# Attention and feed-forward of one chip core: two phases in sequence, or interleaved by hand per batch

## The chip, the core and the metric

The kernel runs on one core of one Trainium2 chip. The core has a matrix engine (PE, with its weight loads shown apart as PEld), a vector engine (DVE), a scalar engine (ACT), a general engine (POOL) and a queue engine (SP) that starts the transfers (DMAs) between the chip's large memory and the core's on-chip memories. Each engine works through its own list of instructions in order and waits at semaphores for the others. The metric is the time of one execution on the device in microseconds (us); smaller is better.

## The reference

Two stages, 4 batches of 768 tokens each, 8 heads of 64 numbers.

```python
q_bits = einsum('bhsd,dk->bhsk', q, proj) > 0        # 6 hash bits per query, the same for keys
mask   = q_bucket[:, :, :, None] == k_bucket[:, :, None, :]
scores = where(mask, 0.125 * q @ k.T, -1e9)          # 768 x 768 per head
attn   = softmax(scores) @ v                         # 768 x 64 per head
x      = attn as (3072 tokens, 512)                  # heads side by side
ffn    = (gelu(x @ w_gate) * (x @ w_val)) @ w_out    # 512 -> 1536 -> 512
out    = x + sigmoid(x @ w_res) * ffn
```

So a query attends only to keys whose 6 bits all equal its own. The kernel (both versions) gets the mask without comparing: the bits are appended to q and k as extra rows of the contraction, scaled so that one bit that differs lowers the exponent far enough for exp to give nothing.

## The kernel before

Every name and line is one of the listing below. The attention comes first, for all four batches, then the feed-forward for all 3072 tokens; the output of the attention, `x_sb`, stays on the chip in between, with the 512 features on the partitions.

For each head, q and k are loaded as 6 tiles of 128 tokens, transposed on PE in fp32 (L104, 6 transposes per side into one PSUM tile `ap`), copied out by ACT (L106), multiplied by `proj` (L109: the 128 tokens are the stationary operand, only 6 columns stream), turned into signs by ACT (L112), transposed again (L116) and copied below the 64 features (L117). DVE makes the bf16 versions (L119, L121). All the PSUM tiles of this preparation have the tag `ap` in a pool with one buffer, so that each step waits until the one before has been copied out.

Then, for each of 6 key tiles `jt`: scores with the keys on the partitions (L134, 512 and 256 queries), exp on ACT in two pieces (L138), and the product with v (L141), v being stationary (65 columns: 64 features and a column of ones that gives the softmax's sum) and the exponentials streaming. The output `ot` has features on the partitions and 768 queries along the row; the sums lie in one row, whose reciprocal (L148) DVE takes on one partition. POOL copies it to 64 partitions (L149) and DVE multiplies (L153).

The feed-forward works on 512 tokens at a time: gate and value products per 128 of the 1536 inner features (L191, L197), GELU on ACT (L194), product on DVE (L199), the gate of the residual (L205, L207 sigmoid), the output product (L213) with features on the partitions, and at the end 16 transposes back (L222, copied by ACT at L223) before the rows are stored (L224). The weights are loaded and cast to bf16 on DVE (L168, L169) when the attention's buffers are given back.

The order of the instructions on each engine is set by a scheduler, from the order of the code and the buffers of the pools. All DMAs go through SP's queue.

## Time and profile before

| | us |
|---|---|
| median of 3 runs | 804.09 (801.24 to 804.7) |
| profiled execution, span from its first to its last instruction | 793.3 |
| its attention, to the last exp | 0 to 534 |
| weights arriving, feed-forward starting | 534 to 600 |
| feed-forward for the rest | 600 to 793 |

| engine | busy us (share of the span) | instructions |
|---|---|---|
| PE | 712.2 (90%) | 3360 |
| PEld | 412.1 (52%) | 3360 |
| DVE | 325.4 (41%) | 383 |
| ACT | 409.0 (52%) | 845 |
| POOL | 37.5 (5%) | 40 |

No time of the profiled execution other than its span is printed; the median of the runs is 10.8 us above that span. Busy time of PE is counted from the start of a matmul to its modelled end, and matmuls overlap: a PE that is busy all the time can still have idle columns. The clock that the throttle granted to PE ("PEclk", 1.00 is full) belongs beside every PE duration: the same matmul streams half as fast at 0.50. The mean over this execution is 0.754. A name such as `sp<-q_aug_bf,k_aug_bf` is output and inputs of an instruction, "PE L134" a line of the listing.

### The profile page before, as it was taken

The page shows a single profiled execution, that of the slowest core. Times are in us where ns is not written, and L with a number is a line of the kernel's source. Part 1 is how long each engine was busy: PE and PEld are TensorE (multiplying, and loading weights), DVE is VectorE, ACT ScalarE, POOL GpSimd, SP SyncE. Part 2 cuts the span into 40 slices and gives each one's busy share as a digit, 9 for nine tenths or more (in the row PEclk, how much of TensorE's full clock was granted, in tenths as well). Part 3 has the DMA queues.
Part 4 walks back from the last instruction along what each step waited for, and adds up shares of the span by engine and source line. Part 5 has one row for each costly group of instructions (what it writes and reads, how often), then busy time and mean ns, then how long its engine had stood idle before and what let it go on. Part 6 is the DMA issues. An engine that isn't in the chain of part 4 may idle for free.

```text
span 793.3 us, 8913 instructions
## 1 busy us (share of the span) xinstructions
PE 712.2 (90%) x3360; PEld 412.1 (52%) x3360; DVE 325.4 (41%) x383; ACT 409.0 (52%) x845; POOL 37.5 (5%) x40
## 2 busy tenths in 40 slices
...
PEclk9965557865567785557675655555899999999997
...
GB/s 141 58 40 41 40 41 30 41 41 40 40 40 39 32 51 40 40 41 30 40 31 31 0 1 1 0 0 283 154 85 61 1 54 0 54 12 43 32 22 54
DMA packets 82299, 36.24 MB, mean 46 GB/s; under 512 B 76112, under 2 KB 76112, under 8 KB 82256
## 3 DMA queue, kind: packets, MB, share of 16 engines
...
## 4 chain that ended last, share of the span: by engine, by line
PE 78%; ACT 10%; issue 6%; DMA 4%; DVE 2%; ACTq 0%; POOL 0%; DVEq 0%; POOLq 0%
PE bp L109 17%; PE ot L141 13%; PE ap L104 10%; PE sp L134 10%; PE fps L213 7%; PE gps L191 7%; PE vps L197 7%; ACT e L138 5%; PE sp_raw L116 5%; DMA tmp<-in_moe_w_out_dram 3%; PE rps L205 2%; ACT k_aug_bf L117 2%; DMA out_dram<-o_row 1%; PE tp L222 1%; ACT q_aug_bf L117 1%
## 5 line engine op out<-in xcount | busy, mean ns | idle before, releaser
L138 ACT ACTIVATE e<-sp,exp_bias_sb 128x512 bf16<-128x512 f32 (+1 forms) x384 | 206.8, 577 | 61.6 <-PE sp L134 57.3
L148 DVE RECIPROCAL recip<-ot 1x512 f32<-1x512 f32 x64 | 160.9, 2532 | 141.9 <-PE ot L141 141.9
L141 PE MATMUL ot<-e,v_aug 128*65 128x512 bf16 (+1 forms) x384 | 166.4, 458 | 26.8 <-ACT e L138 26.8
L134 PE MATMUL sp<-q_aug_bf,k_aug_bf 70*128 70x512 bf16 (+1 forms) x384 | 153.6, 454 | 0.0
L194 ACT ACTIVATE gtmp<-gps 128x512 bf16<-128x512 f32 x72 | 42.9, 597 | 109.8 <-PE gps L191 109.2
L191 PE MATMUL gps<-x_sb,t 128*128 128x512 bf16 x288 | 81.0, 392 | 11.4 <-DVE t L169 9.8
L134 PEld LDWEIGHTS <-k_aug_bf 70*128 70x128 bf16 x384 | 50.3, 131 | 71.8 <-issue 61.3
L197 PE MATMUL vps<-x_sb,t 128*128 128x512 bf16 x288 | 78.5, 389 | 5.8 <-DVE t L169 5.8
L109 PEld LDWEIGHTS bp<-proj_sb,q_aug 64*128 64x128 f32 x384 | 68.8, 271 | 17.5 <-ACT q_aug L106 17.1
L199 DVE TENSOR_TENSOR hh<-gtmp,vps 128x512 bf16<-128x512 bf16 x72 | 49.3, 687 | 69.1 <-PE vps L197 59.9
L141 PEld LDWEIGHTS <-v_aug 128*65 128x65 bf16 x384 | 56.4, 147 | 38.9 <-issue 23.5
L109 PE MATMUL bp<-proj_sb,q_aug 64*128 64x6 f32 x384 | 71.7, 316 | 1.5 <-ACT q_aug L106 1.5
L109 PEld LDWEIGHTS bp<-proj_sb,k_aug 64*128 64x128 f32 x384 | 61.1, 244 | 17.7 <-ACT k_aug L106 17.7
L213 PE MATMUL fps<-hh,t 128*128 128x512 bf16 x288 | 64.7, 382 | 4.3 <-DVE t L169 4.2
L109 PE MATMUL bp<-proj_sb,k_aug 64*128 64x6 f32 x384 | 64.0, 296 | 1.6 <-ACT k_aug L106 1.6
L112 ACT ACTIVATE sgn_t<-bp 128x36 bf16<-128x36 f32 x64 | 12.8, 200 | 94.6 <-PE bp L109 94.6
L149 POOL PARTITION_BROADCAST recip<-recip x32 | 36.4, 1137 | 495.6 <-DVE recip L148 495.6
L104 PE MATMUL ap<-ident,q_s 128*64 128x128 f32 x192 | 46.7, 403 | 14.5 <-POOL ident masks.py:199 9.0
L121 DVE CAST k_aug_bf<-k_aug 64x768 bf16<-64x768 f32 x32 | 18.0, 562 | 83.4 <-ACT k_aug L106 83.4
L191 PEld LDWEIGHTS <-t 128*128 128x128 bf16 x288 | 27.6, 100 | 43.0 <-issue 8.8
L104 PE MATMUL ap<-ident,k_s 128*64 128x128 f32 x192 | 46.7, 405 | 3.4 <-ACT q_aug_bf L117 3.4
L197 PEld LDWEIGHTS <-t 128*128 128x128 bf16 x288 | 27.9, 99 | 40.8 <-DVE t L169 10.1
(34 smaller groups left out, 473.0 us busy)
## 6 DMA issues: line engine op xcount, KB each, us to landing
q_s<-in_q_dram SPq DMA_DIRECT2D x32, 192.0 KB, 2.6
k_s<-in_k_dram SPq DMA_DIRECT2D x32, 192.0 KB, 2.6
v_tmp<-in_v_dram SPq DMA_DIRECT2D x32, 192.0 KB, 3.0
out_dram<-o_row SPq DMA_DIRECT2D x24, 256.0 KB, 2.0
tmp<-in_moe_w_gate_dram SPq DMA_DIRECT2D x4, 768.0 KB, 4.2
tmp<-in_moe_w_val_dram SPq DMA_DIRECT2D x4, 768.0 KB, 4.2
tmp<-in_moe_w_out_dram SPq DMA_DIRECT2D x12, 256.0 KB, 2.7
tmp<-in_moe_w_res_dram SPq DMA_DIRECT2D x4, 256.0 KB, 2.7
```

Source lines behind the costliest of these rows:

```text
L104: nc.tensor.transpose(ap[:D, bass.ts(t, 128)], ten_s[:, t, :], ident)
L109: nc.tensor.matmul(bp[:, t * NBITS:(t + 1) * NBITS], ten_aug[0:D, bass.ts(t, 128)], proj_sb, start=True, stop=True)
L116: nc.tensor.transpose(sp[:NBITS, bass.ts(t, 128)], sgn[:, t, :], ident_bf)
L134: nc.tensor.matmul(sp[:, :nsz], k_aug_bf[0:KAUG, bass.ts(jt, 128)], q_aug_bf[0:KAUG, n0:n0 + nsz], start=True, stop=True)
L138: nc.scalar.activation(e[:, n0:n0 + nsz], sp[:, :nsz], AF.Exp, scale=exp_scale, bias=exp_bias_sb)
L141: nc.tensor.matmul(ot[:, :nsz], v_aug[:, jt, :], e[:, n0:n0 + nsz], start=(jt == 0), stop=(jt == ST - 1))
L148: nc.vector.reciprocal(recip[0:1, n0:n0 + nsz], ot[D:D + 1, :nsz])
L191: nc.tensor.matmul(gps, wg[:, kk, bass.ts(m, P)], x_bf[:, kk, :], start=(kk == 0), stop=(kk == KM - 1))
L194: nc.scalar.activation(gtmp, gps, AF.Gelu)
L197: nc.tensor.matmul(vps, wv[:, kk, bass.ts(m, P)], x_bf[:, kk, :], start=(kk == 0), stop=(kk == KM - 1))
L199: nc.vector.tensor_mul(hh[:, m, :], gtmp, vps)
L213: nc.tensor.matmul(fps, wo[:, kk, bass.ts(m, P)], hh[:, kk, :], start=(kk == 0), stop=(kk == KF - 1))
```

## The change

The kernel is written anew around one loop, and its instructions now stand in the order of the code (`manual_schedule`), not in that of a scheduler.

- **Order.** For each batch b the loop makes 48 steps (8 heads x 6 key tiles). A step issues the scores and the exp of its key tile, then perhaps a piece of the preparation of a later pair of heads, then one or two pieces of the feed-forward of batch b-1 (7 pieces in 4 steps; a batch has 48), and last the product with v of the key tile two steps back. After the 48 steps come 24 transposes of x and the 24 gate products with GELU of batch b; the feed-forward of the last batch stands alone at the end.
- **Preparation** works on a pair of heads. Tokens are loaded 6 neighbours to a partition. Two tiles of 64 features are transposed at once (12 fp32 transposes of 128x128 per pair in place of 24 of 128x64). The hash is one product per head and side with `proj` stationary in 32 columns and 384 token columns streaming (fp32), each of the four on its own 32 columns of PE, that is, on its own 32 output partitions. DVE compares with zero, and 8 small DMAs carry the bit rows below the features (L170).
- **Product with v** (L196): the exponentials are stationary (six 128x128 loads per key tile) and 65 columns of v stream. Tokens are on the partitions, so that the sums are a column: DVE takes 6 reciprocals per partition (L205) and one multiplication (L206). The one-partition reciprocal and the POOL broadcast are gone. `av` has one PSUM buffer.
- **Exp** runs once per key tile over 768 columns without a bias operand (L186); scores have two buffers.
- **Feed-forward** in halves of 384 tokens. Residual gate and output product now give tokens on the partitions (L242, L249), so that the final transposes and their copies are gone; x itself is transposed instead (L215). Sigmoid is written as tanh.
- **Weights** are loaded during batch 0, one transfer every third step, and cast on POOL (L134).

On **SP** the queue at the program's start, before:

```order
L57 DMA proj_sb<-in_proj_dram 64x6
L86 DMA q_s<-in_q_dram 128x6x64
L87 DMA k_s<-in_k_dram 128x6x64
L88 DMA v_tmp<-in_v_dram 128x6x64
L86 DMA q_s<-in_q_dram 128x6x64
```

and now (`aug` is the tile of one head with q and k side by side, `bits` the hash bits of a pair of heads):

```order
L75 DMA proj_pair<-in_proj_dram 64x6
L76 DMA proj_pair<-in_proj_dram 64x6
L101 DMA qs<-in_q_dram 128x2x384
L101 DMA ks<-in_k_dram 128x2x384
L101 DMA vs<-in_v_dram 128x2x384
L170 DMA aug_107<-bits 6x384 x4
L170 DMA aug_110<-bits 6x384 x4
L101 DMA qs<-in_q_dram 128x2x384
```

The loads of one head after the other stood back to back; now the loads of the second pair stand behind the eight transfers that wait for the first pair's hash bits.

On **PE** one key tile in the middle of the attention, before (preparation of later heads between the scores and the product with v):

```order
L134 LDWEIGHTS k_aug_bf
L134 MATMUL sp<-q_aug_bf,k_aug_bf 128x512
L134 LDWEIGHTS k_aug_bf
L134 MATMUL sp<-q_aug_bf,k_aug_bf 128x256
L104 MATMUL ap<-ident,k_s 64x128 x6
L141 LDWEIGHTS v_aug
L141 MATMUL ot<-e,v_aug 65x512
```

and now, at the start of batch 1's steps, behind the last gate product of batch 0 (buffer numbers kept):

```order
L223 MATMUL gps_1287<-xT_1114,wg_147 128x384
L183 LDWEIGHTS aug8_131
L183 MATMUL sc_1293<-aug8_131 128x512
L184 LDWEIGHTS aug8_131
L184 MATMUL sc_1293<-aug8_131 128x256
L233 LDWEIGHTS wv_148
L233 MATMUL vps_1298<-xT_1114,wv_148 128x384
```

Value products of batch 0 now follow the scores of batch 1 on PE, ahead of that key tile's product with v; before, the first product of the feed-forward on PE (L191) stood behind the last one of the attention (L141).

On **ACT**, the same stretch, now (before, all exps of the program came first, then GELU and sigmoid in turns with a table load at each):

```order
L186 ACTIVATE e<-sc 128x768 x16
L225 ACT_TABLE_LOAD
L225 ACTIVATE gh<-gps 128x384 x24
L186 ACT_TABLE_LOAD
L186 ACTIVATE e<-sc 128x768 x6
L152 COPY trT<-tps 128x512
L186 ACTIVATE e<-sc 128x768 x2
L245 ACTIVATE th<-rps 128x512
L186 ACTIVATE e<-sc 128x768 x2
```

Exps, copies of the preparation and tanhs share one order on ACT, and the list holds 8 table loads, two per batch.

The core of the diff (setup, buffers and what is only removed are left out; the removed code is in the listing above):

```diff
+    ctx.enter_context(tc.manual_schedule())
...
+    e_pool = ctx.enter_context(tc.tile_pool(name="e", bufs=6))
+    sc_psum = ctx.enter_context(tc.tile_pool(name="sc_psum", bufs=2, space=PSUM))
+    av_psum = ctx.enter_context(tc.tile_pool(name="av_psum", bufs=1, space=PSUM))
+    mm_psum = ctx.enter_context(tc.tile_pool(name="mm_psum", bufs=3, space=PSUM))
...
+    NAUG = 12
+    augs = []
+    for i in range(NAUG):
+        a = const.tile([P, 2 * S], BF16, name=f"aug{i}")
+        nc.vector.memset(a[D:KAUG, 0:S], 1.0)
+        nc.vector.memset(a[D:KAUG, S:2 * S], -0.25 * NBITS)
+        augs.append(a)
...
+    def load_pair(b, j):
+        for nm, src in (("q", q), ("k", k), ("v", v)):
+            s = stage.tile([P, 2, T, D], FP32, tag=nm + "s", name=nm + "s")
+            nc.sync.dma_start(
+                s, src[b, 2 * j:2 * j + 2].rearrange("h (p t) d -> p h t d", t=T))
+            staged[(nm, b, j)] = s
...
+    def load_weight():
+        nxt = next(weight_gen, None)
+        if nxt is None:
+            return
+        dst, src, parts = nxt
+        tmp = wstage.tile([P, DFF], FP32, tag="wtmp", name="wtmp")
+        if parts is None:
+            view = tmp
+        else:
+            view = tmp[:, :parts * DMODEL].rearrange("p (c d) -> p c d", c=parts)
+        nc.sync.dma_start(view, src)
+        nc.gpsimd.tensor_copy(dst, view)
...
+    def prep_pair(b, j):
+        qs, ks, vs = (staged.pop((nm, b, j)) for nm in "qkv")
+        va = vaugs[b % NVA]
+        nc.gpsimd.tensor_copy(va[:, 2 * j:2 * j + 2, :, 0:D], vs)
+        trT = tr_pool.tile([P, 2 * S], FP32, tag="trT", name="trT")
+        tiles = [s[:, hh, 2 * t2:2 * t2 + 2, :].rearrange("p t d -> p (t d)")
+                 for hh in range(2) for s in (qs, ks) for t2 in range(T // 2)]
+        for g in range(3):
+            ps = mm_psum.tile([P, 512], FP32, tag="mm", name="tps")
+            for i in range(4):
+                nc.tensor.transpose(ps[:, i * P:(i + 1) * P], tiles[4 * g + i], ident)
+            if g == 1:
+                nc.vector.tensor_copy(trT[:, g * 512:(g + 1) * 512], ps)
+            else:
+                nc.scalar.copy(trT[:, g * 512:(g + 1) * 512], ps)
+            yield
+        hp = mm_psum.tile([P, 512], FP32, tag="mm", name="hps")
+        for i in range(4):
+            nc.tensor.matmul(hp[32 * i:32 * i + 32, 0:CH], proj_pair, trT[:, i * CH:(i + 1) * CH],
+                             start=True, stop=True)
+        bits = s_pool.tile([P, CH], BF16, tag="bits", name="bits")
+        nc.vector.tensor_scalar(bits, hp[:, 0:CH], 0.0, 0.5, op0=ALU.is_gt, op1=ALU.subtract)
+        for hh in range(2):
+            a = aug_of(b, 2 * j + hh)
+            for par in range(2):
+                nc.vector.tensor_scalar_mul(
+                    a[0:D, :].rearrange("d (s n) -> d s n", s=2)[:, :, par * CH:(par + 1) * CH],
+                    trT[par * D:(par + 1) * D, hh * S:(hh + 1) * S].rearrange("d (s n) -> d s n", s=2),
+                    QKS)
+            for side in range(2):
+                for par in range(2):
+                    row = 32 * (2 * hh + side) + NBITS * par
+                    nc.sync.dma_start(
+                        a[D:D + NBITS, side * S + par * CH:side * S + (par + 1) * CH],
+                        bits[row:row + NBITS, :])
+        yield
...
+    def scores(b, h, jt):
+        a = aug_of(b, h)
+        sp = sc_psum.tile([P, 1024], FP32, tag="sc", name="sc")
+        lhsT = a[0:KAUG, S + jt * P:S + (jt + 1) * P]
+        nc.tensor.matmul(sp[:, 0:512], lhsT, a[0:KAUG, 0:512], start=True, stop=True)
+        nc.tensor.matmul(sp[:, 512:S], lhsT, a[0:KAUG, 512:S], start=True, stop=True)
+        e = e_pool.tile([P, S], BF16, tag="e", name="e")
+        nc.scalar.activation(e, sp[:, 0:S], AF.Exp, scale=EXPS)
+        e_tiles[(b, h, jt)] = e
+    def attend(b, h, jt):
+        e = e_tiles.pop((b, h, jt))
+        if jt == 0:
+            av_tiles[(b, h)] = av_psum.tile([P, 512], FP32, tag="av", name="av")
+        av = av_tiles[(b, h)]
+        va = vaugs[b % NVA]
+        for t in range(T):
+            nc.tensor.matmul(av[:, t * DV:t * DV + D + 1], e[:, t * P:(t + 1) * P], va[:, h, TS[jt], :],
+                             start=(jt == 0 and t == 0), stop=(jt == T - 1),
+                             skip_group_check=True)
+        if jt == T - 1:
...
+            o = av[:, 0:T * DV].rearrange("p (t d) -> p t d", d=DV)
...
+            rec = s_pool.tile([P, T, 1], FP32, tag="rec", name="rec")
+            nc.vector.reciprocal(rec, o[:, :, D:D + 1])
+            nc.vector.tensor_mul(x_tok[b][:, :, h * D:(h + 1) * D], o[:, :, 0:D],
+                                 rec.to_broadcast([P, T, D]))
+    def transpose_x(b):
+        xT[b] = x_pool.tile([P, KM, S], BF16, tag="xT", name="xT", bufs=1)
+        for ko in range(KM):
+            ps = mm_psum.tile([P, 1024], BF16, tag="mm", name="xps")
+            for t in range(T):
+                nc.tensor.transpose(ps[:, t * P:(t + 1) * P], x_tok[b][:, t, ko * P:(ko + 1) * P], ident_bf)
+            nc.vector.tensor_copy(xT[b][:, ko, :], ps[:, 0:S])
+    def gate(b, m, c):
+        if m == 0:
+            gh[(b, c)] = h_pool.tile([P, KF, CH], BF16, tag="gh", name="gh", bufs=3)
+        ps = mm_psum.tile([P, 512], FP32, tag="mm", name="gps")
+        for kk in range(KM):
+            nc.tensor.matmul(ps[:, 0:CH], wg[:, kk, m * P:(m + 1) * P], xT[b][:, kk, c * CH:(c + 1) * CH],
+                             start=(kk == 0), stop=(kk == KM - 1))
+        nc.scalar.activation(gh[(b, c)][:, m, :], ps[:, 0:CH], AF.Gelu)
+    def feed_forward(b):
+        for c in range(2):
+            for m in range(KF):
+                ps = mm_psum.tile([P, 512], FP32, tag="mm", name="vps")
+                for kk in range(KM):
+                    nc.tensor.matmul(ps[:, 0:CH], wv[:, kk, m * P:(m + 1) * P],
+                                     xT[b][:, kk, c * CH:(c + 1) * CH],
+                                     start=(kk == 0), stop=(kk == KM - 1))
+                sl = gh[(b, c)][:, m, :]
+                nc.vector.tensor_mul(sl, ps[:, 0:CH], sl)
+                yield 4 * CH
+            for t in range(c * T // 2, (c + 1) * T // 2):
+                rps = mm_psum.tile([P, 512], FP32, tag="mm", name="rps")
+                for kk in range(KM):
+                    nc.tensor.matmul(rps, xT[b][:, kk, t * P:(t + 1) * P], wr[:, kk, :],
+                                     start=(kk == 0), stop=(kk == KM - 1))
+                th = o_pool.tile([P, DMODEL], BF16, tag="th", name="th")
+                nc.scalar.activation(th, rps, AF.Tanh, scale=0.5)
+                yield 4 * 512
+                ops = mm_psum.tile([P, 512], FP32, tag="mm", name="ops")
+                for kk in range(KF):
+                    nc.tensor.matmul(ops, gh[(b, c)][:, kk, (t - c * T // 2) * P:(t - c * T // 2 + 1) * P], wo[:, kk, :],
+                                     start=(kk == 0), stop=(kk == KF - 1))
+                    if kk % 4 == 3 and kk < KF - 1:
+                        yield 4 * 512
+                y = o_pool.tile([P, DMODEL], FP32, tag="y", name="y")
+                nc.vector.scalar_tensor_tensor(y, th, 1.0, ops, op0=ALU.add, op1=ALU.mult)
+                o = o_pool.tile([P, DMODEL], FP32, tag="o", name="o")
+                nc.vector.scalar_tensor_tensor(o, y, 0.5, x_tok[b][:, t, :], op0=ALU.mult, op1=ALU.add)
+                nc.sync.dma_start(
+                    out[b * S:(b + 1) * S, :].rearrange("(p t) d -> p t d", t=T)[:, TS[t], :], o)
+                yield 4 * 512
+    for j in range(NPAIR):
+        load_pair(0, j)
+        if j < 2:
+            for _ in prep_pair(0, j):
+                pass
...
+    for b in range(B):
+        todo = list(preps) if b == 0 else []
+        if b + 1 < B:
+            todo += [(b + 1, j) for j in range(NPAIR)]
+        loads = [x for x in todo if x[0] > 0]
...
+        for i in range(nsteps + LEAD):
+            if i < nsteps:
+                scores(b, *bsteps[i])
+            if i % 3 == 0:
+                load_weight()
+            if loads and i % 8 == 2:
+                load_pair(*loads.pop(0))
+            if prep_gen is None and todo and i >= 4 and todo[0] not in loads:
+                prep_gen = prep_pair(*todo.pop(0))
+            if prep_gen is not None and (b == 0 or i % 2 == 1):
+                if not run(prep_gen):
+                    prep_gen = None
+            if ff is not None:
+                run(ff)
+                if i % 4 != 0:
+                    run(ff)
+            if i >= LEAD:
+                attend(b, *bsteps[i - LEAD])
+        while prep_gen is not None or todo:
+            if prep_gen is None:
+                if todo[0] in loads:
+                    load_pair(*loads.pop(0))
+                prep_gen = prep_pair(*todo.pop(0))
+            if not run(prep_gen):
+                prep_gen = None
+        while ff is not None and run(ff):
+            pass
+        transpose_x(b)
+        for c in range(2):
+            for m in range(KF):
+                gate(b, m, c)
+        ff = feed_forward(b)
+    while run(ff):
+        pass
```

220 lines of the change are left out of this document (64 added, 156 removed).

## The prediction

> **What bounds the kernel now.** I read the page first: the slices, then the chain of waits.
>
> ```profile
> PEclk9965557865567785557675655555899999999997
> PE 78%; ACT 10%; issue 6%; DMA 4%; DVE 2%; ACTq 0%; POOL 0%; DVEq 0%; POOLq 0%
> PE bp L109 17%; PE ot L141 13%; PE ap L104 10%; PE sp L134 10%; PE fps L213 7%; PE gps L191 7%; PE vps L197 7%; ACT e L138 5%; PE sp_raw L116 5%; DMA tmp<-in_moe_w_out_dram 3%; PE rps L205 2%; ACT k_aug_bf L117 2%; DMA out_dram<-o_row 1%; PE tp L222 1%; ACT q_aug_bf L117 1%
> ```
>
> PE ends the program, most of it in attention, and the three preparation lines (L109, L104, L116) hold 32%. The clock row matters as much: the attention runs near half clock, the feed-forward at full. By stages:
>
> ```profile
> core 0: us, PE busy (x) PEld busy (x) DVE busy (x) ACT busy (x) POOL busy (x), PEclk, DMA share, GB/s
> 30.00:484.00 454.00, 430.17 (x2120) 282.45 (x2118) 205.71 (x223) 280.74 (x572) 30.63 (x27) 0.67 0.15 35
> 484.00:534.00 50.00, 38.75 (x111) 16.37 (x109) 24.19 (x18) 29.02 (x55) 4.19 (x4) 0.50 0.00 0
> 534.00:560.00 26.00, 8.88 (x19) 1.60 (x18) 13.94 (x13) 2.51 (x4) 1.56 (x1) 0.50 0.76 253
> 611.00:770.00 159.00, 157.59 (x770) 72.65 (x768) 53.44 (x75) 67.87 (x146) 0.00 (x0) 1.00 0.07 27
> ```
>
> From 484 no preparation is left, and the timeline shows attention alone:
>
> ```profile
> 486.92 1.05 ACT L138 ACTIVATE e<-sp,exp_bias_sb 128x512 bf16<-128x512 f32 x2 [0.80 <-PE sp L134]
> 488.04 0.63 PE L134 MATMUL sp<-q_aug_bf,k_aug_bf 70*128 70x512 bf16 x1
> 488.68 0.42 PE L134 MATMUL sp<-q_aug_bf,k_aug_bf 70*128 70x256 bf16 x1
> 488.77 1.05 ACT L138 ACTIVATE e<-sp,exp_bias_sb 128x512 bf16<-128x512 f32 x2 [0.80 <-PE sp L134]
> ```
>
> A key tile takes 1.85 us (488.77 − 486.92). Of it PE streams 1536 columns, 1.28 us at half clock, and the clock stays at 0.50: 69% of half-rate streaming, 0.35 of the full rate, earns no full clock. The dense feed-forward has it all the time. Nothing of the one stage fills the holes of the other; that is what the change can take.
>
> **Prices of the new stream, at full clock.**
>
> ```profile
> 770.00 10.52 PE L213 MATMUL fps<-hh,t 128*128 128x512 bf16 x48
> 308.50 0.50 PE L116 MATMUL sp_raw<-ident_bf,sgn_t 128*6 128x128 bf16 x6
> L116 PE MATMUL sp_raw<-ident_bf,sgn_t x384: 218/268/314, 14.4 to 483.9; 128*6 128x128 bf16 x192
> L213 PEld LDWEIGHTS <-t 128*128 128x128 bf16 x288 | 27.9, 98 | 39.7 <-DVE t L169 6.8 <-issue 0.3
> 9.00 1.49 PE L104 MATMUL ap<-ident,q_s 128*64 128x128 f32 x6 [9.00 <-POOL ident masks.py:199]
> L104 PE MATMUL ap<-ident,q_s x192: 272/421/423, 9.0 to 473.0; 128*64 128x128 f32 x192
> L109 PE MATMUL bp<-proj_sb,q_aug 64*128 64x6 f32 x384 | 71.7, 316 | 1.5 <-ACT q_aug L106 1.5
> ```
>
> - 512 bf16 columns: (10.52 − 0.38)/47 = 0.216 us, 0.422 ns a column, loads hidden. 128 columns: (0.50 − 0.22)/5 = 0.056.
> - Feed-forward of one batch: gate, then 48 pieces of value (24 × 4 × 384 columns), residual (24 × 512) and output (72 × 512), 86,016 columns: **36.3 us**; gate 36,864: 15.6.
> - Scores of a key tile, 768 columns: 0.324. Product with v: six loads of 128 and six streams of 65. Below, the streaming alone, 0.027; above, load and stream in line, 0.098 + 0.027 = 0.125. I take 0.045, a little under the measured 0.056 for twice the columns: 0.27 per key tile.
> - fp32 transposes: (1.49 − 0.42)/5 = 0.214 at half clock, 0.107 at full; 12 per pair: 1.3 us (before 24).
> - Hash: the 384 instructions of L109 are 192 products, two passes each; by the 0.107 for 128 columns one pass over 384 is 0.32, a product 0.64. Four at once 0.64, in line 2.56. I take the middle, 1.6. A pair costs 2.9.
>
> ```profile
> L138 ACT ACTIVATE e<-sp,exp_bias_sb 128x512 bf16<-128x512 f32 x192 | 131.9, 687 | 61.6 <-PE sp L134 57.3 <-PE ap L104 0.7
> L138 ACT ACTIVATE e<-sp,exp_bias_sb 128x256 bf16<-128x256 f32 x192 | 89.6, 466 | 0.0
> L194 ACT ACTIVATE gtmp<-gps 128x512 bf16<-128x512 f32 x72 | 42.9, 597 | 109.8 <-PE gps L191 109.2
> L194 ACT ACT_TABLE_LOAD x6 | 7.7, 1283 | 23.0 <-issue 22.9
> L153 DVE TENSOR_TENSOR x_sb<-ot,recip 64x512 bf16<-64x512 f32 x32 | 21.9, 684 | 12.3 <-POOL recip L149 11.6
> L153 DVE TENSOR_TENSOR x_sb<-ot,recip 64x256 bf16<-64x256 f32 x32 | 13.0, 407 | 0.0
> L119 DVE TENSOR_SCALAR q_aug_bf<-q_aug 64x768 bf16<-64x768 f32 x32 | 19.1, 596 | 56.3 <-ACT q_aug L106 56.3
> ```
>
> - One exp over 768: 687 + 221 = 908 ns, less the 90 that GELU without a bias operand saves (687 − 597) = 0.82; neighbours overlap by 0.1 (1.05 for two of 0.687 and 0.466). I take 0.78.
> - DVE per head: reciprocals 0.1, multiplication over 384 about 0.55 (L153 gives 1.08 ns an element), hand-overs 0.3. `av` has one buffer, so in a stretch without feed-forward pieces PE waits about 0.75 per head before the next product with v may start; queued behind it are the next scores, and ACT waits for those.
>
> **The sum, stage by stage.**
>
> ```profile
> 1.35 0.57 SPq L86 DMA_DIRECT2D q_s<-in_q_dram  x1
> 8.66 0.28 POOL masks.py:199 TENSOR_SCALAR_AFFINE_SELECT ident<-ident 128x128 f32<-128x128 f32 x1 [7.59 <-issue]
> 17.63 0.37 SPq L87 DMA_DIRECT2D k_s<-in_k_dram  x1
> q_s<-in_q_dram SPq DMA_DIRECT2D x32, 192.0 KB, 2.6
> proj_sb<-in_proj_dram SPq DMA_DIRECT2D x1, 1.5 KB, 1.9
> tmp<-in_moe_w_gate_dram SPq DMA_DIRECT2D x4, 768.0 KB, 4.2
> out_dram<-o_row SPq DMA_DIRECT2D x24, 256.0 KB, 2.0
> ```
>
> 1. *Start, 30.* Transposes begin at 9.0 as before. Pair 0: transposes and copies to 12.6, the last hash products at half clock to 15.6, bits at 16.2. Eight bit transfers at 0.4 of SP each: 19.5. Only behind them come the loads of pair 1, two issues (1.0) and a landing (2.6) later, at 23; its hash ends at 29.7, and only then does PE come to the scores. The bits of pair 0, landing 1.9 after their issue, are long there.
> 2. *Batch 0, 64.* 4 plain steps 3.4; 30 steps with preparation, PE being last: (5 × 0.594 + 2.9) × 6 = 35.4; 14 plain steps at 0.78, ACT being last, 10.9; half clock at first 5; `av` waits 3; loads of later pairs that stand on SP behind weight loads, two stalls of 3.
> 3. *Four batch ends, 92.* From the last product with v: 0.65 on DVE, six transposes and hand-over 0.55, four copies of 768 on DVE at 0.96, hand-overs 0.4: PE idle 5.4. Then gate 15.6, and 2 for a clock that falls in the hole. Both table loads (1.28 us each) lie in the hole or beside the first pieces of feed-forward.
> 4. *Batches 1 and 2, 80 each.* 28 mixed steps: 28 × 0.594 + 36.3 + 2.5 pairs × 2.9 = 60.2, PE last throughout. 20 steps without feed-forward: 15.6 + 2.3 for `av` + 1.5 for the preparation.
> 5. *Batch 3, 71*, without preparation: 52.9 + 17.9.
> 6. *End, 40*: the last 48 pieces 36.3, then two DVE passes of 0.68 (as L153) and a store of 2.0.
>
> Sum 457. I add 4%, between the 1% of PE's idle time in 611 to 770 and the 5% in 30 to 484, for hand-overs that I don't list: 475 as span. The median of the runs shown, 804.09, stands 10.8 over the profiled span 793.3; with the same, **485**.
>
> Costed at nothing: tanh (24 × 0.6 on ACT, hidden under 0.86 and 2.6 us of products); value products' multiplication on DVE (0.55 a piece of 0.65 to 0.86); four scalings per pair on DVE (0.6 each by L119, beside PE's 2.9 and five steps); and the weight casts, now on POOL:
>
> ```profile
> L169 DVE CAST t<-tmp 128x1536 bf16<-128x1536 f32 x8 | 7.6, 950 | 10.0 <-DMA tmp<-in_moe_w_val_dram 5.2 <-DMA tmp<-in_moe_w_gate_dram 4.7
> ```
>
> Between DVE's 0.95 and 3.4 (POOL's 282 ns for 128 elements above, twelvefold), two buffers and 4.2 us of landing make at most 3.8 per load, 14 loads 53 us, done at about 90, before batch 0 ends at 94; gate needs only the first four. At 10 us a cast the cover is gone: the pair loads queued behind on SP come some 20 us late, and PE stands.
>
> On the clock. In 484 to 534 half clock persists with no long hole in PE's work. The Trainium skill ("TensorE: Matmul & The Clock Gate", Part 1) says that about 3.4 us of sustained work releases the full clock and an idle window takes it away; the values 0.50 and 1.00 agree, but by its advice on holes alone 484 to 534 should have run at full. So the density of columns decides here: 0.35 of the full rate isn't enough, 1.0 is. The plain steps stream 1158 columns (0.49 us) per 0.78, 0.62 of the full rate, and 0.49 per 1.19 at half clock, 0.41: the worst place, and the ground of rival B.
>
> **The rivals.**
>
> - *A, the sum*, 0.60: 455 to 520.
> - *B, half clock wherever no feed-forward runs*, 0.14. Then a plain step is 0.65 + 0.54 = 1.19, five with preparation 11.7 in place of 5.9: batch 0 +37, batches 1 and 2 +11 each, batch 3 +8: **552**. For it: 484 to 534. Against it: preparation makes PE last there, and PE then never waits.
> - *C, the weight loads show*, 0.15: 0.125 per pair in place of 0.045, +0.48 per key tile where PE is last (84 mixed and 30 preparation steps, 55 us), +0.29 in the 78 others (23): **562**. For it: 98 ns a load. Against it: L116 and L213 hide theirs. The Trainium skill ("TensorE: Matmul & The Clock Gate", Back-to-back issue gap) gives 81 ns for a load with 128 columns; L116's 56 beats it. By 81 the time would be some 513.
> - *D, less than the sum*, 0.08: 0.030 per pair, hash four at once, no unlisted 4%: **442**.
> - *E, the other side*, 0.03: the gate grants half clock throughout, since 65-column matmuls thin out every stretch. PE's work at full clock is 62 + 52 + 207 (feed-forward) + 21 + 26 + 5 = 373; at half 747, and with the rest of the start 19, four holes 22, end 4 and `av` 10 the span is 802, the time **813**. It decides once the mean clock falls under 0.51. Against it: mixed steps stream over 0.9 of the full rate.
>
> The Trainium skill ("TensorEngine Tiling (Array Packing)", Key Properties) also says that a change of tiling mode drains PE. No row shows one; with L116's 0.22 for one matmul's depth, 32 changes would be an estimate of 7 us.
>
> **The numbers.** 485; 440 to 575 holds A to D but for tails. A measurement here tells 0.5%, 4 us. Faster 0.97 (A to D and a part of E), within 0.5% 0.01, slower 0.02.
>
> **What would show it.** In the profile after: scores of batch 1 between value products at clock 1.00; a first exp near 30 us; exps 0.73 to 0.82; `av` matmuls starting 30 to 60 ns apart; holes of about 5 us before each gate block. Wrong would be: clock 0.50 in batch 0 beyond its first steps or behind step 28 of a batch (B), `av` pairs over 0.1 us (C), PE waiting for `qs` or weights over 10 us, four hash products over 2.6 us.

## The result and the profile after

The changed kernel takes **468.8 us** (median of 4 runs, 467.8 to 469.5), the kernel before 804.06 beside it: a ratio of 0.583, 95% interval 0.581 to 0.585. Forecast were 485, with 440 to 575 as the range. The profiled execution took 469.5, its span 467.4. Medians in this text are of all runs of a kernel; ratios leave out runs that took over 1.5% longer than its fastest.

From the page of the changed kernel: PE's busy time, the clock slices, and the chain by engine and by line.

```profile
PE 389.1 (83%) x3104; PEld 231.1 (49%) x3104; DVE 189.8 (41%) x347; ACT 237.0 (51%) x352; POOL 36.2 (8%) x38
PEclk9998787679999999979999999977999999999999
PE 68%; DVE 16%; DMA 5%; ACT 5%; issue 3%; SPq 3%; ACTq 0%; DVEq 0%
PE ops L249 13%; PE gps L223 13%; PE vps L233 10%; PE sc L183 7%; PE av L196 7%; PE tps L148 5%; PE rps L242 4%; DMA ks<-in_k_dram 4%; ACT e L186 4%; DVE aug L163 4%; PE sc L184 3%; PE hps L156 3%; DVE xtok L206 3%; SPq L170 2%; DVE aug L83 2%
```

PE's busy time fell from 712 to 389 us. The feed-forward (L249, L223, L233) is now the largest part of the chain, and the preparation (L148, L156) has 8% where L109, L104 and L116 had 32%. The mean clock rose from 0.754 to 0.936. What is new is DVE with 16% (2% before) and SP's queue with 3%; DMA has 5% in place of 4%. These are the waits that the forecast either did not price or priced too low.

The stages, as windows of the changed kernel (columns: stretch and length, busy time of PE, PEld, DVE, ACT and POOL with instructions, clock, DMA share, GB/s):

```profile
core 0: us, PE busy (x) PEld busy (x) DVE busy (x) ACT busy (x) POOL busy (x), PEclk, DMA share, GB/s
0.00:38.20 38.20, 11.13 (x41) 5.33 (x41) 21.10 (x34) 3.62 (x5) 2.79 (x10) 1.00 0.19 63
38.20:120.50 82.30, 55.47 (x509) 34.93 (x508) 29.83 (x55) 43.33 (x61) 23.31 (x19) 0.79 0.61 211
120.50:138.50 18.00, 17.52 (x122) 10.80 (x120) 2.61 (x6) 12.17 (x24) 2.80 (x3) 1.00 0.28 96
138.50:195.00 56.50, 55.76 (x448) 32.16 (x446) 30.15 (x55) 30.05 (x41) 2.21 (x2) 1.00 0.23 75
195.00:221.00 26.00, 19.42 (x214) 12.78 (x213) 9.94 (x19) 17.44 (x24) 0.98 (x1) 0.85 0.12 43
340.40:408.40 68.00, 64.19 (x580) 37.35 (x579) 26.39 (x50) 42.79 (x57) 0.00 (x0) 1.00 0.07 24
426.40:467.40 41.00, 36.49 (x193) 18.58 (x190) 21.27 (x36) 4.07 (x7) 0.00 (x0) 0.98 0.11 39
```

They are the start, batch 0, its end with the gate, the mixed and the plain steps of batch 1, batch 3, and the end. In the mixed stretch PE is idle 0.7 of 56.5 us at full clock; in batch 0 it is idle 27 of 82, and in the plain steps of batch 1 it is idle 6.6 of 26. The clock of 1.00 printed for the start is not what its matmuls show: six hash passes take 1.50 there (L156, below), where eight take 0.90 at full clock.

| stage | forecast | measured |
|---|---|---|
| start, to the first scores | 30 | 38.2 |
| batch 0 | 64 | 82.3 |
| four batch ends | 92 | 73 |
| batches 1 and 2 | 160 | 165 |
| batch 3 | 71 | 68 |
| end | 40 | 41 |
| 4% unlisted, then time outside the span | 18 + 10.8 | 0 + 2.1 |

The forecast's column adds up to 485.8, which it wrote as 485.

The start, by the timeline of the changed kernel (start, length, engine, line; in brackets the idle time before):

```profile
5.60 0.87 PE L148 MATMUL tps<-ident,qs 128*128 128x128 f32 x3 [5.60 <-DMA qs<-in_q_dram]
19.68 0.70 DVE L83 MEMSET aug<- 7x768 bf16 x1
20.54 0.89 DVE L150 COPY trT<-tps 128x512 f32<-128x512 f32 x1 [0.16 <-issue]
21.48 1.50 PE L156 MATMUL hps<-trT,proj_pair 128*32 128x384 f32 x6 [11.03 <-DVE trT L150]
23.62 5.82 SPq L170 DMA_DIRECT2D aug<-bits  x8
29.49 0.45 SPq L101 DMA_DIRECT2D qs<-in_q_dram  x1
```

Twenty-four memsets of constant rows stand on DVE from 1.1 to 20.4 us, ahead of the one copy for the hash that DVE makes (L150; ACT makes the other two). Then eight bit transfers hold SP for 5.82 us, 0.73 each, and only behind them comes the load of pair 1. The Trainium skill ("VectorE: DVE Perf Modes", Zero memsets can be issued as uint32) says that a memset takes one cycle per element whatever the type. The trace shows one type at this length, 698 ns for 768 bf16 elements (0.91 each), and so can't test that.

The largest waits of PE in the changed kernel (total, times, longest):

```profile
PE tps L148 <- DMA qs<-in_q_dram: 30.6, 5, 10.0
PE av L196 <- DVE xtok L206: 23.8, 20, 3.4
```

The longest wait of the second kind, DVE and PE in the changed kernel at a head's end in batch 1:

```profile
199.14 2.78 DVE L163 TENSOR_SCALAR aug<-trT 64x768 bf16<-64x768 f32 x4
201.84 0.18 DVE L205 RECIPROCAL rec<-av 128x6 f32<-128x6 f32 x1
202.06 0.56 DVE L206 TENSOR_TENSOR xtok<-av,rec 128x384 bf16<-128x384 f32 x1
202.67 0.51 PE L196 MATMUL av<-vaug,e 128*128 128x65 bf16 x6 [3.43 <-DVE xtok L206]
```

The division of the finished head waits on DVE behind four scalings of the preparation, and PE 3.43 us for the division. Six `av` products took 0.34 to 0.36 before that wait and 0.51 to 0.54 after it, at half clock.

### The profile page after: what moved, and what is told of

It reads as the page before. It is cut to its first block, busy times and chain, and to the rows that moved or that the text cites. A ratio compares the mean times of both kernels' runs of the same rounds, so it can differ in the third digit from the quotient of the medians.

```text
span 467.4 us, 7688 instructions
## 1 busy us (share of the span) xinstructions
PE 389.1 (83%) x3104; PEld 231.1 (49%) x3104; DVE 189.8 (41%) x347; ACT 237.0 (51%) x352; POOL 36.2 (8%) x38
## 4 chain that ended last, share of the span: by engine, by line
PE 68%; DVE 16%; DMA 5%; ACT 5%; issue 3%; SPq 3%; ACTq 0%; DVEq 0%
PE ops L249 13%; PE gps L223 13%; PE vps L233 10%; PE sc L183 7%; PE av L196 7%; PE tps L148 5%; PE rps L242 4%; DMA ks<-in_k_dram 4%; ACT e L186 4%; DVE aug L163 4%; PE sc L184 3%; PE hps L156 3%; DVE xtok L206 3%; SPq L170 2%; DVE aug L83 2%
## 5 line engine op out<-in xcount | busy, mean ns | idle before, releaser
L186 ACT ACTIVATE e<-sc 128x768 bf16<-128x768 f32 x192 | 150.4, 811 | 106.1 <-PE sc L184 106.1
L196 PEld LDWEIGHTS <-e 128*128 128x128 bf16 x1152 | 63.1, 103 | 64.8 <-DVE xtok L206 24.5
L196 PE MATMUL av<-vaug,e 128*128 128x65 bf16 x1152 | 71.7, 202 | 25.3 <-DVE xtok L206 23.8
L237 DVE TENSOR_TENSOR gh<-vps,gh 128x384 bf16<-128x384 f32 x96 | 52.9, 557 | 91.2 <-PE vps L233 87.1
L183 PE MATMUL sc<-aug 71*128 71x512 bf16 x192 | 78.4, 408 | 4.4 <-ACT e L186 3.4
L249 PE MATMUL ops<-wo,gh 128*128 128x512 bf16 x288 | 70.0, 379 | 0.0
L233 PE MATMUL vps<-xT,wv 128*128 128x384 bf16 x384 | 69.8, 326 | 0.1
L223 PE MATMUL gps<-xT,wg 128*128 128x384 bf16 x384 | 64.7, 329 | 0.4 <-DVE xT L216 0.2
L225 ACT ACTIVATE gh<-gps 128x384 bf16<-128x384 f32 x96 | 47.0, 490 | 25.2 <-PE gps L223 25.2
L184 PE MATMUL sc<-aug 71*128 71x256 bf16 x192 | 55.4, 289 | 0.0
L223 PEld LDWEIGHTS <-wg 128*128 128x128 bf16 x384 | 37.8, 99 | 26.3 <-issue 2.4
L233 PEld LDWEIGHTS <-wv 128*128 128x128 bf16 x384 | 37.3, 97 | 24.5 <-issue 0.3
L148 PE MATMUL tps<-ident,qs 128*128 128x128 f32 x96 | 23.6, 341 | 30.6 <-DMA qs<-in_q_dram 30.6
L249 PEld LDWEIGHTS <-gh 128*128 128x128 bf16 x288 | 27.9, 97 | 31.0 <-issue 1.2
L150 DVE COPY trT<-tps 128x512 f32<-128x512 f32 x16 | 11.3, 703 | 55.6 <-PE tps L148 55.4
L148 PEld LDWEIGHTS tps<-ident,qs 128*128 128x128 f32 x96 | 15.2, 177 | 37.1 <-issue 18.8
L141 POOL CAST vaug<-vs 128x768 bf16<-128x768 f32 x16 | 15.1, 944 | 200.9 <-DMA vs<-in_v_dram 150.0
L156 PE MATMUL hps<-trT,proj_pair 128*32 128x384 f32 x128 | 19.5, 572 | 11.0 <-DVE trT L150 11.0
```

What stands on the lines that cost most here:

```text
L148: nc.tensor.transpose(ps[:, i * P:(i + 1) * P], tiles[4 * g + i], ident)
L156: nc.tensor.matmul(hp[32 * i:32 * i + 32, 0:CH], proj_pair, trT[:, i * CH:(i + 1) * CH], start=True, stop=True)
L183: nc.tensor.matmul(sp[:, 0:512], lhsT, a[0:KAUG, 0:512], start=True, stop=True)
L184: nc.tensor.matmul(sp[:, 512:S], lhsT, a[0:KAUG, 512:S], start=True, stop=True)
L186: nc.scalar.activation(e, sp[:, 0:S], AF.Exp, scale=EXPS)
L196: nc.tensor.matmul(av[:, t * DV:t * DV + D + 1], e[:, t * P:(t + 1) * P], va[:, h, TS[jt], :], start=(jt == 0 and t == 0), stop=(jt == T - 1),
```

## The experiments

Every kernel was timed against the kernel before on the same chip. The chips differ: the kernel before took 797 to 804 us on them, so a difference of a few us between two rows says little without the windows.

| kernel | us, median | ratio to before, 95% |
|---|---|---|
| the change | 468.8 | 0.583 (0.581 to 0.585) |
| feed-forward apart | 499.9 | 0.625 (0.619 to 0.631) |
| hash in line | 490.2 | 0.613 (0.606 to 0.619) |
| memsets on POOL | 455.7 | 0.570 (0.565 to 0.576) |
| bits by POOL | 445.3 | 0.557 (0.553 to 0.562) |
| one piece per step | 455.9 | 0.575 (0.571 to 0.579) |
| preparation last | 456.4 | 0.576 (0.571 to 0.581) |
| before, hash alone | 646.0 | 0.813 (0.806 to 0.821) |
| before, token-major alone | 798.6 | 1.007 (1.003 to 1.011) |
| before, both | 675.9 | 0.840 (0.834 to 0.846) |
| before, both and exps whole | 635.7 | 0.779 (0.772 to 0.786) |
| four edits together | 414.6 | 0.516 (0.514 to 0.519) |
| the four and two `av` buffers | 409.3 | 0.511 (0.507 to 0.514) |

**What interleaving is worth.** The pieces of feed-forward move from the steps to behind the gate.

```diff
-            if ff is not None:
-                run(ff)
-                if i % 4 != 0:
-                    run(ff)
...
         ff = feed_forward(b)
-    while run(ff):
-        pass
+        while run(ff):
+            pass
```

> The 48 feed-forward pieces of batch b run whole right behind its gate, none between the steps of batch b+1; all else as in the changed kernel. Mine (the sum of streams): PE is last in either order, so little is lost: 28 steps per batch that took 0.594 us of PE each now take the pace of the exps, 0.72, 3.5 us more, and five heads per batch wait for av 1 us each in the open: 8 to 10 us for each of three batches, 27 together, 490 to 500 us. Rival 1 (without pieces between them those steps fall to half clock, 0.97 a step): 10.5 + 5 per batch, 47 together, about 515. Rival 2 (the interleaving is what earns most of the 335 us): 570 or more.

499.9: 31 us more, so by far the most of the 335 us is not the interleaving. (That is what it is worth in the changed kernel; interleaving alone was not put into the kernel before.) The attention of batches 0, 1 and 3 in that run:

```profile
37.70:119.10 81.40, 55.69 (x506) 34.99 (x505) 29.50 (x55) 43.36 (x61) 22.22 (x18) 0.77 0.60 214
173.70:232.90 59.20, 46.27 (x464) 29.58 (x463) 20.21 (x40) 41.11 (x57) 3.70 (x4) 0.82 0.27 88
400.90:438.70 37.80, 31.15 (x388) 19.75 (x386) 6.65 (x16) 35.53 (x49) 0.00 (x0) 1.00 0.03 8
```

With its 36.7 us of pieces batch 1 takes 95.9, 13 more than in the change, and batch 3 takes 74.5, 6.5 more. The 13 lie above my 8 to 10, and the clock of 0.82 points to a part of rival 1. Batch 3, without preparation, holds full clock with no pieces at all.

**Four column tiles.** The hash on the whole array, one product after the other:

```diff
-            nc.tensor.matmul(hp[32 * i:32 * i + 32, 0:CH], proj_pair, trT[:, i * CH:(i + 1) * CH],
-                             start=True, stop=True)
+            nc.tensor.matmul(hp[:, 0:CH], proj_wide[i], trT[:, i * CH:(i + 1) * CH],
+                             start=(i == 0), stop=(i == 3))
```

> The four hash products of a pair on the whole array, one after the other into the same rows (the projection at columns 32i of a wide stationary that is zero elsewhere); one exp buffer fewer to make room for it. Mine (four column tiles run together): a product is two passes over 384 columns, 0.32 us each at full clock, so four in line take 2.56 in place of the 0.65 now seen, 1.9 more per pair; twice that for the two pairs at the start at half clock (7.6), 6 pairs in batch 0 (11, less what the waits for loads hide), 8 in batches 1 and 2 (15, less what lies under ACT): 20 to 34 us, about 495 us, and the hash products of a pair 2.6 us or more from first start to last. Rival (the tiles run one after the other and the short time has another reason): 469, no change.

490.2, 21 us more, 4.3 of them before the first scores (42.5 for 38.2). The wide stationaries also cost one of six exp buffers, and POOL writes them in the first 5 us. The eight passes of one pair at full clock in the timeline of the change:

```profile
197.72 0.90 PE L156 MATMUL hps<-trT,proj_pair 128*32 128x384 f32 x8
```

and in that of the hash in line:

```profile
169.77 2.74 PE L162 MATMUL hps<-trT,proj_wide 128*128 128x384 f32 x8
```

So four column tiles run together: 0.90 against 2.74, latency included.

**The start.** Eight of the twelve tiles get their constant rows from POOL.

```diff
-        nc.vector.memset(a[D:KAUG, 0:S], 1.0)
-        nc.vector.memset(a[D:KAUG, S:2 * S], -0.25 * NBITS)
+        eng = nc.vector if i < 4 else nc.gpsimd
+        eng.memset(a[D:KAUG, 0:S], 1.0)
+        eng.memset(a[D:KAUG, S:2 * S], -0.25 * NBITS)
```

> The constant rows of the last eight of twelve augmented tiles are written by POOL, not by DVE. Mine: 24 memsets of 0.7 us stand on DVE until 20.4 us, ahead of the one copy of a transposed block that DVE has; with 8 left it comes at some 8 us, PE's 11.0 us wait in front of the first hash goes, and the first scores come 11 earlier: 458 us. Rival (the start is set by the loads of pair 1 behind the bit transfers on SP, or by POOL, which now has the memsets ahead of the casts of v): 466 to 469, a gain under 3.

455.7, 13 less. In this run's timeline the hash no longer waits (11.0 us in the change), and the first scores stand at 25.4 instead of 38.2:

```profile
7.89 0.69 DVE L151 COPY trT<-tps 128x512 f32<-128x512 f32 x1
8.68 2.19 PE L157 MATMUL hps<-trT,proj_pair 128*32 128x384 f32 x8
25.42 0.39 PE L184 MATMUL sc<-aug 71*128 71x512 bf16 x1
```

**The bit transfers.** They go through POOL's queue.

```diff
-                    nc.sync.dma_start(
+                    nc.gpsimd.dma_start(
                         a[D:D + NBITS, side * S + par * CH:side * S + (par + 1) * CH],
```

> The eight small transfers of hash bits per pair are issued by POOL, not by SP. Mine: each block of eight holds SP 5.6 to 8.9 us and the loads of later pairs stand behind it; without that the loads of pair 1 are issued at once (first scores some 8 us earlier), and most of PE's 30.6 us of waits for loads in batch 0 goes, some 20: 438 to 448 us. Rival 1 (the loads of weights, not the bits, hold the pair loads): 465. Rival 2 (POOL's issues cost more than SP's and its casts of v stand behind them): 469 or more.

445.3, 23 less, the largest single gain. In this run PE's wait for loads, and SP and POOL at the start:

```profile
PE tps L148 <- DMA qs<-in_q_dram: 5.5, 1, 5.5
23.91 4.66 POOL L170 DMA_DIRECT2D aug<-bits  x8 [13.73 <-DVE bits L159]
28.30:96.20 67.90, 53.28 (x506) 34.34 (x507) 34.12 (x54) 43.46 (x61) 55.69 (x78) 0.80 0.66 225
```

The wait fell from 30.6 to 5.5 us; the first scores stand at 28.3, and batch 0 takes 67.9 instead of 82.3. The weights' transfers go through SP as before, so it was the bits that held the loads. They held them in two ways. In the changed kernel SP spends 0.73 to start each of the 128 transfers, some 93 us in all. And it stands still until the bits are there, with the loads behind them:

```profile
SPq L170 <- DVE bits L159: 78.6, 11, 19.8
```

The longest of these waits lies between the loads of pair 0 and the first bits at 23.62; with the bits on POOL the loads of pair 1 are issued at 3.8. No run separates the two ways. The Trainium skill ("DMA: Bandwidth & Descriptors", Issuing engines are not separate DMA queues) says that starting DMAs from several engines saves only the sequencer's time, usually small beside the transfer. Here the move saved 23 us of the program, the wait in order included. The Trainium skill ("DMA: Bandwidth & Descriptors", SWDGE vs HWDGE vs iDMA) gives the path from POOL the slower setup. The issue alone took less there, 0.58 (4.66 / 8) against 0.73; from issue to landing it took 2.6 (median) on POOL's queue, and no run shows that time for SP.

**Plain steps filled.** One piece in every step:

```diff
                 run(ff)
-                if i % 4 != 0:
-                    run(ff)
```

> The changed kernel with one feed-forward piece in every step instead of seven in four steps: 48 pieces over the 50 steps of a batch, so no step is left without. Mine: PE's streams of a batch are 48 x 0.594 for the steps, 36.3 for the pieces and 4 x 2.1 for the preparation, 73 us; with no plain steps left nothing is to wait for exps, and batches 1 and 2, 82.5 each now, come to about 74, batch 3 from 68 to 65: 20 us less, 445 to 452 us, and the clock stays full through batches 1 to 3. Rival 1 (the steps with preparation are held by DVE and av, not by the lack of pieces): 460 to 469. Rival 2 (feed-forward now ends later than the last step of attention and the batch end grows): 470 or more.

455.9, 13 less, between mine and rival 1, so neither figure was met. Batch 1 of this run as a window:

```profile
135.70:213.20 77.50, 71.98 (x653) 42.82 (x657) 38.56 (x73) 48.20 (x65) 1.66 (x2) 0.98 0.15 51
```

77.5 in place of 82.5, at a clock of 0.98. With batch 2 (77.6 for 82.2) and batch 3 (65.1 for 68.0) the windows give 12.5 of the 13. PE is still idle 5.5 us, 4.4 of them in five waits for divisions.

**Divisions ahead of scalings.** Within a step the pieces and the product with v come first, the preparation last:

```diff
-            if prep_gen is None and todo and i >= 4 and todo[0] not in loads:
-                prep_gen = prep_pair(*todo.pop(0))
-            if prep_gen is not None and (b == 0 or i % 2 == 1):
-                if not run(prep_gen):
-                    prep_gen = None
...
             if i >= LEAD:
                 attend(b, *bsteps[i - LEAD])
+            if prep_gen is None and todo and i >= 4 and todo[0] not in loads:
+                prep_gen = prep_pair(*todo.pop(0))
+            if prep_gen is not None and (b == 0 or i % 2 == 1):
+                if not run(prep_gen):
+                    prep_gen = None
```

> The changed kernel with the preparation piece last in a step, behind the feed-forward pieces and the product with v, so that the reciprocal and multiplication of a head's end stand on DVE ahead of the preparation's four scalings of 0.6 us. Mine: most of PE's 23.8 us of waits for those two goes, 10 to 15 us: 454 to 460 us. Rival 1 (the head's end meets the scalings in few steps, or the preparation's own products now come later and hold the next loads): 466 to 472.

456.4, 12 less; batches 1 and 2 take 76.0 and 76.1. PE's wait for the divisions halved, and on DVE (around the same head's end) the division is ahead:

```profile
PE av L196 <- DVE xtok L206: 12.8, 14, 4.0
194.21 0.56 DVE L206 TENSOR_TENSOR xtok<-av,rec 128x384 bf16<-128x384 f32 x1
195.26 2.66 DVE L163 TENSOR_SCALAR aug<-trT 64x768 bf16<-64x768 f32 x4
```

**Where most of the 335 us comes from.** Parts of the change were put alone into the kernel before. First the hash:

```diff
-                    for t in range(ST):
-                        nc.tensor.matmul(bp[:, t * NBITS:(t + 1) * NBITS],
-                                         ten_aug[0:D, bass.ts(t, 128)], proj_sb,
+                    for (n0, nsz) in NCH:
+                        nc.tensor.matmul(bp[:NBITS, n0:n0 + nsz],
+                                         proj_sb, ten_aug[0:D, n0:n0 + nsz],
...
-                    nc.scalar.activation(sgn[:, :], bp[:, :ST * NBITS], AF.Sign)
...
-                    for t in range(ST):
-                        nc.tensor.transpose(sp[:NBITS, bass.ts(t, 128)], sgn[:, t, :], ident_bf)
-                    nc.scalar.copy(ten_aug_bf[D:KAUG, :], sp[:NBITS, :S])
+                    nc.scalar.activation(ten_aug_bf[D:KAUG, :], bp[:NBITS, :S], AF.Sign)
```

> The kernel before with its hash alone changed: the projection is the stationary operand and 768 tokens stream past it, and the sign is written straight to the rows it belongs in; the six small products, the sign in token-major and the six transposes back go. Mine: L109's products hold 136 us of PE and L116 some 40; the new ones take 64 x 768 columns x 2 passes at half clock, 83 us: 90 us less on PE, and two hand-overs fewer per tensor, so 700 to 720 us. Rival 1 (these products lie beside other work): 790. Rival 2 (the hand-overs between PE and ACT were the larger part): 640 to 690.

646.0, about 151 us less: beyond my 700 to 720 and at rival 2's figure, though its reason, the hand-overs, is not what the rows show most of. L109 and L116 held PE 179 us, the new products (L107) hold it 102. The clock slices, and the groups of the scores and the product with v, which the edit doesn't touch:

```profile
PEclk9999999999999999999996555699899999999998
L134 PE MATMUL ot<-e,v_aug 128*65 128x512 bf16 (+1 forms) x384 | 125.0, 356 | 30.5 <-ACT e L131 30.5
L127 PE MATMUL sp<-q_aug_bf,k_aug_bf 70*128 70x512 bf16 (+1 forms) x384 | 115.7, 356 | 0.0
```

In the kernel before these same matmuls took:

```profile
L141 PE MATMUL ot<-e,v_aug 128*65 128x512 bf16 (+1 forms) x384 | 166.4, 458 | 26.8 <-ACT e L138 26.8
L134 PE MATMUL sp<-q_aug_bf,k_aug_bf 70*128 70x512 bf16 (+1 forms) x384 | 153.6, 454 | 0.0
```

The clock rose from 0.754 to 0.935, and the untouched scores and products with v lost 38 and 41 us of busy time with it. The likely reading: the small products held PE with 6 columns each, which counts as busy in the trace and didn't hold the clock. Holes in PE's work don't explain the lower clock before: in the attention with preparation PE was busy 430 of 454 us then, and 311 of 360 now (first window below). Still, the edit changed products and hand-overs together, so that the cause of the higher clock is argued, not shown. With tokens streaming the stretch holds full clock, until in the last attention steps (slices 22 to 25) no preparation is left.

Then the token-major output, in the kernel before:

```diff
-                    for (ot, n0, nsz) in ots:
-                        nc.tensor.matmul(ot[:, :nsz],
-                                         v_aug[:, jt, :],
-                                         e[:, n0:n0 + nsz],
-                                         start=(jt == 0), stop=(jt == ST - 1))
+                    for t in range(ST):
+                        nc.tensor.matmul(ot[:, t * DV:t * DV + D + 1],
+                                         e[:, bass.ts(t, 128)], v_aug[:, jt, :],
+                                         start=(jt == 0 and t == 0), stop=(jt == ST - 1),
+                                         skip_group_check=True)
...
-                nc.gpsimd.partition_broadcast(recip[:, :], recip[0:1, :])
...
+                nc.vector.reciprocal(rec, o[:, :, D:D + 1])
+                nc.vector.tensor_mul(x_tok[:, :, h * D:(h + 1) * D], o[:, :, 0:D],
+                                     rec.to_broadcast([128, ST, D]))
...
+                for t in range(ST):
+                    nc.tensor.transpose(xp[:, bass.ts(t, 128)], x_tok[:, t, ko * 128:(ko + 1) * 128], ident_bf)
```

> The kernel before with its attention output alone changed to token-major: exps are the stationary operand, 65 columns of v stream, one division per head on 128 partitions, x transposed once per batch; no reciprocal on one partition and no broadcast on POOL. Mine: at half clock the product with v takes some 0.33 us per key tile in place of 0.69, 0.3 less for 192 key tiles, 60 us; half of it is under ACT's exps, and the 16 transposes and copies per batch take some 10 back: 760 to 785 us. Rival 1 (ACT and the hand-overs set the step of 1.85 us, nothing to gain): 795 to 810. Rival 2 (thinner streaming lets the clock fall further, or DVE's reciprocals of 2.5 us were on the path): beyond either end, over 815 or under 740.

798.6: no gain (ratio 1.007) where I expected 760 to 785. It is the figure of rival 1, but not for its reason: near the end of the attention a key tile takes 1.66 us in this run, by two of ACT's rows, where it took 1.85.

```profile
502.06 1.05 ACT L136 ACTIVATE e<-sp,exp_bias_sb 128x512 bf16<-128x512 f32 x2 [0.61 <-PE sp L132]
503.72 1.05 ACT L136 ACTIVATE e<-sp,exp_bias_sb 128x512 bf16<-128x512 f32 x2 [0.61 <-PE sp L132]
```

What was won there was lost in the clock: in this run the untouched hash products (L109) hold PE 155 us in place of 136, and the scores 165 in place of 154. Both parts together:

> The kernel before with both parts: the hash with tokens streaming and the token-major attention output. With the hash alone the clock in the stretch with preparation was 0.94, with the token-major output alone 0.60 (before 0.67). Mine: at full clock ACT sets the pace (0.80 busy in 30 to 390 us of the run with the hash alone), so the shorter products with v bring little: 630 to 650 us beside 646 with the hash alone. Rival 1 (now that PE runs at full clock the 0.15 to 0.3 us less per key tile come through): 590 to 615. Rival 2 (the thinner streaming takes the clock back down): 680 or more.

And both with each exp in one instruction:

```diff
-                    for (n0, nsz) in NCH:
-                        sp = score_psum.tile([128, 512], FP32, tag="sp")
-                        nc.tensor.matmul(sp[:, :nsz],
+                    sp = score_psum.tile([128, 1024], FP32, tag="sp")
+                    for (n0, nsz) in NCH:
+                        nc.tensor.matmul(sp[:, n0:n0 + nsz],
...
-                        nc.scalar.activation(e[:, n0:n0 + nsz], sp[:, :nsz], AF.Exp,
-                                             scale=exp_scale, bias=exp_bias_sb)
+                    nc.scalar.activation(e, sp[:, 0:S], AF.Exp,
+                                         scale=exp_scale, bias=exp_bias_sb)
```

> The same kernel with both parts and each exp over 768 columns in one instruction instead of 512 and 256; the banks for it are those that the token-major output gives back. Mine (ACT sets the pace): 1.05 us per key tile become 0.82, 192 x 0.23 = 44 us less than the run with both parts, about 595 to 610. Rival (PE or the hand-overs set the pace): within 10 us of the run with both parts.

675.9, some 30 us *more* than the hash alone (21 by the ratios, as the chips differ): close to rival 2's figure of 680, with its reason. Most of the attention, as windows of three kernels, first the kernel with the hash alone:

```profile
30.00:390.00 360.00, 311.16 (x1363) 129.47 (x1362) 227.59 (x242) 287.03 (x561) 37.33 (x31) 0.94 0.19 43
```

with the token-major output alone:

```profile
30.00:530.00 500.00, 468.88 (x3018) 336.58 (x3018) 67.79 (x193) 297.65 (x611) 0.00 (x0) 0.60 0.14 31
```

and with both:

```profile
30.00:400.00 370.00, 326.79 (x2086) 141.66 (x2083) 66.77 (x188) 271.51 (x531) 0.00 (x0) 0.76 0.18 41
```

Token-major takes the clock from 0.67 to 0.60 in the kernel before, and from 0.94 to 0.76 with the new hash: 390 columns stream per key tile where 768 did, and the clock falls with them. Whole exps, for which the token-major output gives back the banks, bring 40 us by the medians (635.7) and 49 by the ratios, about the 44 expected, though from a base 30 us higher than mine. That figure is soft: the runs of these two kernels scatter by 1.7% and 4.6%.

**Together.** The four edits of the start, the bits, the pieces and the order, and then two buffers for `av`:

> The changed kernel with four edits together that brought 13, 23, 13 and 12 us alone: constant rows of eight tiles written by POOL, bit transfers issued by POOL, one feed-forward piece per step, preparation last in a step. Mine: the start falls from 38 to some 15 us, 13 more in batch 0, and the last two share what they gain in batches 1 to 3 (both fill or shorten the same waits): 18 for 25; 410 to 420 us. Rival 1 (the four are independent): 407 or less. Rival 2 (POOL with memsets, casts of v, casts of weights and the bit transfers becomes late): 430 or more.

```diff
-    av_psum = ctx.enter_context(tc.tile_pool(name="av_psum", bufs=1, space=PSUM))
-    mm_psum = ctx.enter_context(tc.tile_pool(name="mm_psum", bufs=3, space=PSUM))
+    av_psum = ctx.enter_context(tc.tile_pool(name="av_psum", bufs=2, space=PSUM))
+    mm_psum = ctx.enter_context(tc.tile_pool(name="mm_psum", bufs=2, space=PSUM))
```

> The four edits together with two buffers for av and two in place of three for all other products. Mine: the remaining waits for the last head's division, some 8 to 12 us, go, and two buffers are enough where pieces of 0.65 us or more alternate: 5 to 10 us less than the four edits alone. Rival (two buffers hold the transposes and pieces, each waiting for its copy): 5 to 30 us more.

414.6 and 409.3, both as expected. Windows of the four edits together (start, batch 0, batch 1):

```profile
0.00:20.70 20.70, 8.51 (x40) 4.25 (x40) 14.57 (x23) 3.62 (x5) 19.90 (x36) 0.93 0.85 292
20.70:86.40 65.70, 53.76 (x506) 35.10 (x507) 31.68 (x50) 43.48 (x61) 53.11 (x75) 0.79 0.69 226
104.90:177.60 72.70, 70.26 (x655) 42.91 (x659) 38.40 (x73) 47.95 (x65) 20.57 (x35) 1.00 0.17 54
```

Batch 1 takes 72.7 us, the 73 that PE's streams alone add up to. Of the start I expected 15 and got 20.7: POOL is busy 19.9 of it with memsets, casts and transfers, the bits wait their turn there, and PE waits 3.9 us for them. The second `av` buffer ends PE's waits for divisions and shortens batch 0 to 57 us; with one buffer fewer for the other products each batch end takes about 1 us more. At 409 us this version takes 0.51 of the time before, and beats both kernels.

## Why the prediction was right, and where its parts were not

The sum of streams held: PE is last in the mixed steps (55.8 of 56.5 us busy at full clock), and 467.4 of span stand against 475. But that the number came so close is partly luck, as two groups of errors met. The start (+8), batch 0 (+18), batches 1 and 2 (+5) and the end (+1) were too cheap; the batch ends (−19), batch 3 (−3), the unlisted 4% (−18) and the time outside the span (−9) too dear. 33 against 49: the difference is the 16 us by which the forecast lies above.

- *Start, 30 → 38.2.* The step "transposes and copies to 12.6" left out the memsets ahead of DVE's copy; taking them away brought 13 us. Transposes began at 5.6, not 9.0. The transfers of the bits cost 0.73 of SP, not 0.4, which delayed pair 1 as the step said, 2.6 us further.
- *Batch 0, 64 → 82.3.* The term "two stalls of 3" for loads was mis-sized: of the 30.6 us that PE waited for `qs`, 5.6 are the program's first load, 10.0 pair 1's, and 15.0 lie here, in three waits. "`av` waits 3" measured 8.9, in five. I had the queue right and the culprit wrong: the bits stand ahead of the loads, not the weights. "Half clock at first" was too short as well: 0.79 over the whole batch. The bits by POOL alone brought this batch to 67.9.
- *Batch ends, 92 → 73.* The term "PE idle 5.4" was too large: from the last product with v to the first of the gate are 1.8 to 2.4 us with the transposes in them, because the copies run beside the transposes and take 0.55 us each, not 0.96 (group below). The longest gate block took 16.7 us against 16.1 at full clock, so little of the 2 us for the clock was needed.
- *Time outside the span, 10.8 → 2.1.* The 10.8 set one execution's span beside the median of other executions. Where a run of the kernel before lists both, time and span lie 1.9 apart (794.0 and 792.1).

The copies of xT as a group of the changed kernel, and with them exps, casts and products with v:

```profile
L216 DVE COPY xT<-xps 128x768 bf16<-128x768 bf16 x16 | 8.3, 552 | 0.3
L186 ACT ACTIVATE e<-sc 128x768 bf16<-128x768 f32 x192 | 150.4, 811 | 106.1 <-PE sc L184 106.1
L134 POOL CAST wg<-wtmp 128x1536 bf16<-128x1536 f32 x4 | 6.0, 1498 | 28.5 <-DMA wtmp<-in_moe_w_gate_dram 28.5
L196 PE MATMUL av<-vaug,e 128*128 128x65 bf16 x1152 | 71.7, 202 | 25.3 <-DVE xtok L206 23.8
```

- *Batches 1 and 2, 80 → 82.5.* The mixed 28 steps took 56.5, not 60.2 (cheaper hash and pairs); the plain 20 took 26, not 19.4. The term "2.3 for `av`" missed that the divisions queue behind the scalings on DVE, 2.78 us of them; I had costed those scalings at nothing beside PE's work and named no one waiting behind them. Putting the preparation last brought 12 us.
- *Unit prices.* The pair of the product with v: 0.028 ((0.34 − 0.20) / 5), at the lower bound, not 0.045; the loads hide. (The forecast leaned on L116 for that, whose loads have 6 columns, not 128; in the changed kernel L215 loads 128 columns for every 128 that it streams, and its pace is 0.056, (1.17 − 0.22) / 17.) Hash per pair 0.90 with its latency against 1.6. Exp 0.81, its pace 0.70 ((3.62 − 0.81) / 4) against 0.78. POOL's casts 1.5, between the bounds, and covered as foreseen.

The rows for those on PE and ACT, from the changed kernel's timeline:

```profile
39.05 3.62 ACT L186 ACTIVATE e<-sc 128x768 bf16<-128x768 f32 x5 [2.33 <-PE sc L184]
40.94 0.34 PE L196 MATMUL av<-vaug,e 128*128 128x65 bf16 x6
120.35 1.17 PE L215 MATMUL xps<-ident_bf,xtok 128*128 128x128 bf16 x18
```

- *The rivals.* C fell with the 0.028 per pair. The Trainium skill ("TensorE: Matmul & The Clock Gate", Back-to-back issue gap) gives 81 ns for a load and a matmul of 128 columns, which the forecast turned into 513 us; L215's 56 ns for that pair is below it. B, half clock wherever no feed-forward runs, is wrong as a rule (batch 3 without pieces ran at 1.00) but right in part: in batch 0 and behind the long divisions of batches 1 and 2 the clock fell. D had the prices right (0.028, hash four at once, no 4%), and was kept from being the result by the start and batch 0: with the bits alone out of the way the time is 445. E fell. A drain at a change of tiling isn't excluded, but it must fit, with the latency, into the 0.26 us between the eight passes' 0.90 and two full passes of 0.32 each.
- *The signs named.* Scores between value products at clock 1.00 were there, exps at 0.81, in range. The first exp at 39 us, the holes of 2 us, `av` matmuls 28 ns apart, PE waiting for `qs` 30.6 us and half clock in part of the steps behind step 28 were not as foreseen; the last two were on the list of what would be wrong.
- *What the forecast's argument lacked.* It took the gain to be "the holes of the other stage" filled. Interleaving brought 31 us. The hash alone, in the old kernel, brought 151, of which the untouched scores and products with v show 79 as the clock rose. How the rest divides (tiles of two heads, exps in one piece, weights loaded beside the attention) was tried only for the exps, 40 to 49, and for the column tiles, 21; these shares overlap and don't add up to 335.
